# Six cross layers on one core: two more row quads biased on VectorE, and the fifth layer's products made one feature tile at a time

## The chip, the cores and the metric

The kernel runs on one core of one Trainium2 chip. The metric is the device time of one execution in microseconds, as the median of several runs; a single execution was recorded by the hardware profiler, and all views below are of that one.

## What is computed

A stack of six cross layers on 4096 rows with 416 features, all in bf16:

```python
B, F, D, L = 4096, 26, 16, 6          # features: F * D = 416
def reference(x0, ws, bs):            # x0 [4096, 416], ws [6, 416, 416], bs [6, 416]
    x = x0
    for l in range(ws.shape[0]):
        x = x0 * (x @ ws[l] + bs[l]) + x
    return x
```

Every layer multiplies by `x0` and adds the last `x`, so `x` is always `x0` times a factor: with c = 1 at first, each layer does c += x @ w + b and x = x0 * c. The kernel keeps that factor c (tiles `CM` and `CR`) and adds to it.

## The kernel before

**Layout.** In layers one to five everything is transposed: features on the partitions, rows along them. 416 features are three full tiles of 128 (m = 0, 1, 2) and a remainder of 32. The 4096 rows are two halves (s = 0, 1) of 2048, each four groups g of 512 columns. `XM0` is the transposed input, `XH` three rotating buffers for the transposed x of a half, `CM` the factor of the full tiles; the remainder lies in `XR` and `CR`, with the four groups of a half stacked on four blocks of 32 partitions. A feature tile of one half is 128 x 2048 elements, made as two pieces of 1024.

**A layer.** TensorE makes the sums of a tile (`mm_full`, L208, and the remainder's share in `mm_row`, L214) into two PSUM buffers of 1024 columns. ScalarE evicts each with the layer's bias (L187, or `evict`, L332, in layer five) into a buffer `t` (six of them). VectorE then does the addition to the factor (L188, or `add`, L340) and the product with `XM0` that gives the next x (L189, or `mul`, L344). There are six tiles a layer, called A, Bt, C (first half, m = 0 to 2) and Dt, E, F (second half).

**Layer five** is `feeding_layer` (L325). It has an order of its own, written out by hand from L381 to L427; `pin` keeps VectorE's instructions in the order of the text. Besides additions and products, it turns the factor back into rows for layer six: `rows_out` (L350) issues a DMA transpose of a finished tile of `CM` on SP's queue (`xl_dmat`, L231) into `XLrows`, and `rem_out` (L375) the same for the remainder by way of `scrR`, from where ScalarE copies it (`xl_rem`, L311). For the first half, `last_bias` (L347) adds the bias of layer six to the factor ahead of the transpose, after the tile's product was made. For the second half nothing is added, and the transpose is issued as soon as the additions are done.

**Layer six** (L450 on) works by rows: the output of 128 rows is a "unit" of 128 x 416 in PSUM. A quad q = (s, i) is the four units of i-th 128 columns of the four groups; so there are eight quads, and 32 units. Rounds of two quads each fill four PSUM tiles. `mm_q_rem` (L477) makes the remainder's share of a quad, four matmuls on four row groups (L480). In the second half (`if s`), four more matmuls of one row of ones with the bias (L484) put the bias into PSUM, as the transposed factor doesn't hold it. Then ScalarE casts the sums to `t` (L509), VectorE adds the rows of the factor (L511) and multiplies by `X0rows` (L499), and the output is issued on SP's queue (L500). At the very end, for the last three units, TensorE adds the factor itself by products with the identity (L472, L474), and the last unit is multiplied straight from PSUM and stored from ScalarE's queue.

SP's queue holds, in order of the text: the loads of the start, the eight transposes of layer five, and 22 of the 23 outputs.

Of the kernel before, what the change touches and what calls it, by code (L numbers as in the profile page):

```python
# [10 lines left out]
ALU = mybir.AluOpType  # L11
# [5 lines left out]
def kernel(  # L17
# [7 lines left out]
    nc = tc.nc  # L25
    B, D = x0.shape
    L = ws.shape[0]
# [4 lines left out]
    NS = 2  # L32
    NG = 4
    CW = 512
    SW = NG * CW
    NBT = B // P
    LL = L - 1
# [14 lines left out]
    WR = const.tile([P, L, D], BF16)  # L52
# [3 lines left out]
    bM = const.tile([P, NK, L], FP32)  # L56
    bR = const.tile([P, L], FP32)
    X0rows = big.tile([P, NBT, D], BF16)
    XLrows = big.tile([P, NBT, D], BF16)
    scrR = [big.tile([P, 4, P], BF16, name=f"scrR{s}") for s in range(NS)]  # L60
# [3 lines left out]
    XM0 = big.tile([P, NK, B], BF16, name="XM0")  # L64
    XH = [big.tile([P, NK, SW], BF16, name=f"XH{i}") for i in range(3)]
    XR = [big.tile([P, NS * CW], BF16, name=f"XR{i}") for i in range(3)]
    CM = big.tile([P, NK, B], BF16, name="CM")
    CR = big.tile([P, NS * CW], BF16, name="CR")

    def col0(s, g):  # L70
        return SW * s + CW * g
# [8 lines left out]
    def pin(ins):  # L80
        tc.keep_in_program_order(ins)
# [136 lines left out]
    def mm_rem(l, s, pr, cur, curR):  # L218
        for g in range(NG):
            nc.tensor.matmul(pr[32 * g:32 * g + 32, :], lhsT=WD[:, l, g, :], rhs=curR[:, CW * s:CW * s + CW],  # L220
                             start=True, stop=False, tile_position=(0, 32 * g))
        for k in range(NK):
            for g in range(NG):
                nc.tensor.matmul(pr[32 * g:32 * g + 32, :], lhsT=WM[:, l, k, NK * P:D], rhs=cur[s][:, k, CW * g:CW * g + CW],  # L224
                      start=False, stop=(k == NK - 1), tile_position=(0, 32 * g))
# [4 lines left out]
    def xl_dmat(s, k):  # L230
        nc.sync.dma_start_transpose(out=XLrows[:, 16 * s:16 * s + 16, 128 * k:128 * k + 128],  # L231
                                    in_=CM[:, k, SW * s:SW * s + SW])
# [73 lines left out]
    def xl_rem(s):  # L306
        dst = XLrows[:, 16 * s:16 * s + 16, NK * P:D].rearrange("p (g i) r -> p i g r", g=NG)
        src = scrR[s][:].rearrange("p i (g r) -> p i g r", g=NG)
        n = 4 if s else 2
        for i in range(0, 4, n):  # L310
            pin(nc.scalar.copy(dst[:, i:i + n], src[:, i:i + n]))  # L311

    def layer_products(l, n, tiles, pts, cur, curR, between):
        ta, tb = tiles[n], tiles[n + 1]
        pts[ta] = new_pts()
        for g in range(NG):
            mm_full(l, ta[0], ta[1], g, pts[ta], cur, True, False)
        mm_row(l, ta[0], ta[1], pts[ta], curR, False, True)
        pts[tb] = new_pts()
        mm_row(l, tb[0], tb[1], pts[tb], curR, True, False)  # L320
        between(ta)
        for g in range(NG):
            mm_full(l, tb[0], tb[1], g, pts[tb], cur, False, True)

    def feeding_layer(l, cur, curR, nxt, nxtR):  # L325
        tiles = [(s, m) for s in range(NS) for m in range(NK)]
        pts, ts = {}, {}

        def evict(t):
            for h in range(2):  # L330
                ts[t + (h,)] = tpool.tile([P, 2 * CW], BF16, name="t")
                nc.scalar.activation(ts[t + (h,)][:], pts[t][h][:].rearrange("p a b -> p (a b)"), ACT.Identity,  # L332
                                     bias=bM[:, t[1], l:l + 1], scale=1.0)

        def c_of(t, h):
            c0 = col0(t[0], 2 * h)
            return CM[:, t[1], c0:c0 + 2 * CW]

        def add(t, h):
            pin(nc.vector.tensor_tensor(out=c_of(t, h), in0=ts[t + (h,)][:], in1=c_of(t, h), op=ALU.add))  # L340

        def mul(t, h):
            c0 = col0(t[0], 2 * h)
            pin(nc.vector.tensor_tensor(out=nxt[t[0]][:, t[1], 2 * CW * h:2 * CW * h + 2 * CW], in0=c_of(t, h),  # L344
                                        in1=XM0[:, t[1], c0:c0 + 2 * CW], op=ALU.mult))

        def last_bias(c, bias):  # L347
            pin(nc.vector.tensor_scalar(out=c, in0=c, scalar1=bias, scalar2=None, op0=ALU.add))

        def rows_out(t):  # L350
            s, m = t
            if s == 0:
                last_bias(CM[:, m, 0:SW], bM[:, m, LL:L])
            xl_dmat(s, m)

        A, Bt, C, Dt, E, F = tiles
        layer_products(l, 0, tiles, pts, cur, curR, evict)
        evict(Bt)
        pr2 = psum.tile([P, 2, CW], FP32, tag="ps", name="pr2")
        for s in range(NS):  # L360
            mm_rem(l, s, pr2[:, s, :], cur, curR)
        tr = []
        for s in range(NS):
            tr.append(tpool.tile([P, 2 * CW], BF16, name="t"))
            for a in range(0, CW, CW // 2):
                nc.scalar.activation(tr[s][:, a:a + CW // 2], pr2[:, s, a:a + CW // 2], ACT.Identity, bias=bR[:, l:l + 1], scale=1.0)

        def rem(s, op):
            part = slice(CW * s, CW * s + CW)
            if op == ALU.add:  # L370
                pin(nc.vector.tensor_tensor(out=CR[:, part], in0=tr[s][:, 0:CW], in1=CR[:, part], op=op))
            else:
                pin(nc.vector.tensor_tensor(out=nxtR[:, part], in0=CR[:, part], in1=XR[0][:, part], op=op))

        def rem_out(s):  # L375
            part = slice(CW * s, CW * s + CW)
            if s == 0:
                last_bias(CR[:, part], bR[:, LL:L])
            nc.sync.dma_start_transpose(out=scrR[s][:], in_=CR[:, part])

        add(A, 0)  # L381
        mul(A, 0)
        add(A, 1)
        add(Bt, 0)
        mul(A, 1)
        rows_out(A)
        add(Bt, 1)
        mul(Bt, 0)
        rem(0, ALU.add)
        mul(Bt, 1)  # L390
        rem(0, ALU.mult)
        rem_out(0)
        rows_out(Bt)
        rem(1, ALU.add)
        rem_out(1)
        rem(1, ALU.mult)

        layer_products(l, 2, tiles, pts, cur, curR, evict)
        evict(Dt)
        add(C, 0)  # L400
        add(C, 1)
        mul(C, 0)
        mul(C, 1)
        rows_out(C)
        add(Dt, 0)
        add(Dt, 1)
        rows_out(Dt)
        mul(Dt, 0)
        mul(Dt, 1)

        def before_last(t):
            xl_rem(0)
            evict(t)

        layer_products(l, 4, tiles, pts, cur, curR, before_last)
        evict(F)
        add(E, 0)
        mul(E, 0)
        add(E, 1)
        rows_out(E)  # L420
        add(F, 0)
        mul(E, 1)
        add(F, 1)
        rows_out(F)
        mul(F, 0)
        mul(F, 1)
        xl_rem(1)  # L427

    cur, curR = XH[0:2], XR[1]
    for l in range(1, LL):  # L430
        nxt, nxtR = [[h for h in XH if h is not cur[0] and h is not cur[1]][0], cur[0]], XR[1 + (l % 2)]
        if l == LL - 1:
            feeding_layer(l, cur, curR, nxt, nxtR)
            cur, curR = nxt, nxtR
            break
        tiles = [(s, m) for s in range(NS) for m in range(NK)]
        pts = {}

        def finish(t):
            for h in range(2):  # L440
                ew_main(l, t[0], t[1], h, pts[t][h], nxt)

        for n in range(0, len(tiles), 2):
            layer_products(l, n, tiles, pts, cur, curR, finish)
            finish(tiles[n + 1])
            if n == 0:
                rem_pair(l, cur, curR, nxtR)
        cur, curR = nxt, nxtR

    l = LL  # L450
# [25 lines left out]

    def mm_q_rem(q, py, done):  # L477
        s, i = quads[q]
        for g in range(NG):
            nc.tensor.matmul(py[g][:, 0:D], lhsT=curR[32 * g:32 * g + 32, CW * s + 128 * i:CW * s + 128 * i + 128],  # L480
                             rhs=WR[32 * g:32 * g + 32, l, :], start=(g >= done), stop=(s == 0 and g < done),
                             tile_position=(32 * g, 0))
        for g in range(NG if s else 0):
            nc.tensor.matmul(py[g][:, 0:D], lhsT=ones[32 * g:32 * g + 1, :],  # L484
                             rhs=bLr[32 * g:32 * g + 1, :], start=False, stop=(g < done), tile_position=(32 * g, 0))

# [88 lines left out]
```

## Time and profile before

| what | us |
|---|---|
| median of three runs | 129.69 |
| runs, lowest to highest | 129.56 to 129.72 |
| the profiled execution | 129.56 |
| its span, first to last instruction | 127.8 |
| TensorE busy in the span | 123.0 |
| VectorE busy in the span | 102.3 |
| ScalarE busy in the span | 87.6 |

The span is what the profile shows; 1.76 us of the execution lie around it. Busy time is the time in which an engine's instructions ran; overlapping ones are counted once. Each row of the order of time has the start, the length, the engine, the line of the kernel, output and inputs by the program's names, the shape and how many instructions are merged in the row; in brackets stands the idle time of the engine ahead of it, and what ended it. PE is TensorE, DVE is VectorE, ACT is ScalarE, SPq the queue of SP. The granted clock of TensorE was 0.999 over the span.

### The profile page before, as it was taken

Reading aid. Unit: us, or ns where it says so; the run is one execution under the profiler, and the core shown is the slowest. Engines: PE = TensorE matmul, PEld = TensorE weight load, DVE = VectorE, ACT = ScalarE, POOL = GpSimd, SP = SyncE. Lnnn points to the kernel's source line nnn. Section 1 sums busy time; section 2 is a strip of 40 time slices with the busy share of each in tenths; the row PEclk is TensorE's granted clock in tenths of the full one; section 3 lists DMA queues with packets and bytes.
Section 4 is the critical chain, followed back from the end, with each engine's and each line's share of the span. In section 5 each row is a group of like instructions: output and inputs, shape, how many; then the busy total and the mean of one; then the engine's idle time right before and its main releaser. Section 6 shows DMA issues by size and latency. Waiting matters only on the chain.

```text
span 127.8 us, 3986 instructions
## 1 busy us (share of the span) xinstructions
PE 123.0 (96%) x1692; PEld 55.5 (43%) x1694; DVE 102.3 (80%) x199; ACT 87.6 (69%) x109; POOL 5.0 (4%) x18
## 2 busy tenths in 40 slices
PE   7999999999999999999999999999999999999980
PEld 3343343444444344534454434443545345445450
DVE  0123569974979898989898989898999999998990
ACT  0038866887858567858577859577859697669660
POOL 4004001400000000000000000000000000000000
PEclk9999999999999999999999999999999999999999
DMA  3999999999950000000000000000078999999964
GB/s 95 237 234 219 178 235 260 310 333 333 339 159 0 5 0 0 8 0 5 0 5 0 5 0 0 5 0 5 0 146 92 183 164 202 165 263 286 311 198 148
DMA packets 42230, 16.38 MB, mean 128 GB/s; under 512 B 31034, under 2 KB 42212, under 8 KB 42212
## 3 DMA queue, kind: packets, MB, share of 16 engines
q1 hardware_dynamic: 37432, 15.40, 52.9%
q10 hardware_dynamic: 4780, 0.72, 3.6%
q8 instruction: 13, 0.21, 0.7%
q14 instruction: 5, 0.04, 0.1%
HBM read 6.15 MB, written 3.41 MB: 75 GB/s over the span
## 4 chain that ended last, share of the span: by engine, by line
PE 90%; DMA 4%; ACTq 2%; DVEq 1%; issue 0%; ACT 0%; DVE 0%
PE pt L208 50%; PE py L468 12%; PE ph L240 11%; PE pt L214 5%; PE pr L224 5%; DMA xrig<-in_x_dram 4%; PE pr L220 2%; PE py L480 2%; PE ph L247 1%; PE py L462 1%; ACTq L86 1%; PE py L484 1%; DVEq L570 1%; ACTq L108 1%; ACT t L509 0%
## 5 line engine op out<-in xcount | busy, mean ns | idle before, releaser
L208 PE MATMUL pt<-XH,WM 128*32 128x512 bf16 x1152 | 65.2, 379 | 0.0
L187 ACT ACTIVATE t<-pt,bM 128x1024 bf16<-128x1024 f32 x36 | 37.1, 1114 | 13.7 <-PE pt L214 13.7
L208 PEld LDWEIGHTS <-WM 128*32 128x32 bf16 x1152 | 29.7, 97 | 33.8 <-issue 5.1
L188 DVE TENSOR_TENSOR CM<-t,CM 128x1024 bf16<-128x1024 bf16 x36 | 24.7, 687 | 4.2 <-ACT t L187 4.2
L189 DVE TENSOR_TENSOR XH<-CM,XM 128x1024 bf16<-128x1024 bf16 x36 | 24.9, 692 | 2.6
L509 ACT CAST t<-py 128x416 bf16<-128x416 f32 (+1 forms) x22 | 14.3, 648 | 4.5 <-PE py L468 2.1
L468 PE MATMUL py<-WM,XH 128*128 128x416 bf16 x90 | 17.0, 339 | 0.0
L240 PE MATMUL ph<-XM,WM 128*128 128x512 bf16 x70 | 16.3, 379 | 0.2
L332 ACT ACTIVATE t<-pt,bM 128x1024 bf16<-128x1024 f32 x12 | 12.4, 1114 | 4.2 <-PE pt L214 4.2
L181 ACT ACTIVATE CM<-ph,bM 128x1024 bf16<-128x1024 f32 x12 | 12.5, 1113 | 3.5 <-PE ph L247 3.5
L183 DVE TENSOR_TENSOR XH<-CM,XM 128x512 bf16<-128x512 bf16 x24 | 9.1, 439 | 3.6 <-ACT CM L181 3.6
L468 PEld LDWEIGHTS <-XH 128*128 128x128 bf16 x90 | 8.5, 98 | 7.5 <-issue 1.2
L240 PEld LDWEIGHTS <-WM 128*128 128x128 bf16 x72 | 6.8, 98 | 8.6 <-issue 1.1
L499 DVE TENSOR_TENSOR o<-t,X0rows 128x416 bf16<-128x416 bf16 (+1 forms) x22 | 9.9, 458 | 0.1
L511 DVE TENSOR_TENSOR t<-t,XLrows 128x416 bf16<-128x416 bf16 (+1 forms) x20 | 9.3, 468 | 0.6 <-ACT t L509 0.6
L340 DVE TENSOR_TENSOR CM<-t,CM 128x1024 bf16<-128x1024 bf16 x12 | 7.9, 685 | 0.3 <-ACT t L332 0.3
L344 DVE TENSOR_TENSOR XH<-CM,XM 128x1024 bf16<-128x1024 bf16 x12 | 8.0, 686 | 0.1
L214 PE MATMUL pt<-XR,WR 32*128 32x512 bf16 x96 | 7.3, 379 | 0.0
L224 PE MATMUL pr<-XH,WM 128*32 128x512 bf16 x96 | 6.6, 379 | 0.0
L196 ACT ACTIVATE t<-pr,bR 128x256 bf16<-128x256 f32 x12 | 4.7, 474 | 1.6 <-PE pr L224 1.6
L114 ACT ACT_TABLE_LOAD x1 | 1.3, 1283 | 6.1 <-DMA XM<-in_x_dram 6.1
L224 PEld LDWEIGHTS <-WM 128*32 128x32 bf16 x120 | 3.2, 97 | 3.2
(61 smaller groups left out, 58.2 us busy)
## 6 DMA issues: line engine op xcount, KB each, us to landing
X0rows<-in_x_dram SPq DMA_DIRECT2D x8, 312.0 KB, 7.0
out_dram<-o SPq DMA_DIRECT2D x9, 208.0 KB, 3.3
WM<-in_ws_dram SPq DMA_DIRECT2D x5, 312.0 KB
out_dram<-o SPq DMA_DIRECT2D x13, 104.0 KB, 1.9
X0rows<-in_x_dram SPq DMA_DIRECT2D x4, 208.0 KB, 6.4
WR<-in_ws_dram SPq DMA_DIRECT2D x4, 130.0 KB, 5.1
WM<-in_ws_dram ACTq DMA_DIRECT2D x1, 312.0 KB
XM<-in_x_dram SPq DMA_TRANSPOSE x8, 5.7
```

What stands on the lines that cost most here:

```text
L181: nc.scalar.activation(c, src, ACT.Identity, bias=bias, scale=1.0)
L187: nc.scalar.activation(t[:], src, ACT.Identity, bias=bias, scale=1.0)
L188: nc.vector.tensor_tensor(out=c, in0=t[:], in1=c, op=ALU.add)
L189: nc.vector.tensor_tensor(out=x, in0=c, in1=XM0[:, m, c0:c0 + 2 * CW], op=ALU.mult)
L208: nc.tensor.matmul(pts[g // 2][32 * q:32 * q + 32, g % 2, :], lhsT=WM[:, l, k, 128 * m + 32 * q:128 * m + 32 * q + 32], rhs=cur[s][:, k, C ...
L214: nc.tensor.matmul(pts[g // 2][:, g % 2, :], lhsT=WR[32 * g:32 * g + 32, l, 128 * m:128 * m + 128], rhs=curR[32 * g:32 * g + 32, CW * s:CW ...
L224: nc.tensor.matmul(pr[32 * g:32 * g + 32, :], lhsT=WM[:, l, k, NK * P:D], rhs=cur[s][:, k, CW * g:CW * g + CW], start=False, stop=(k == NK ...
L240: nc.tensor.matmul(pt[:, gl, :], lhsT=WM[:, 0, k, 128 * m:128 * m + 128], rhs=cur[:, k, c0:c0 + CW], start=(k == 0 and not after_row), sto ...
L332: nc.scalar.activation(ts[t + (h,)][:], pts[t][h][:].rearrange("p a b -> p (a b)"), ACT.Identity, bias=bM[:, t[1], l:l + 1], scale=1.0)
L468: nc.tensor.matmul(py[:, 0:D], lhsT=q_x(q, g, k), rhs=WM[:, l, k, :], start=((not closes) and k == 0), stop=(closes and not adds and k == ...
L499: pin(nc.vector.tensor_tensor(out=o[:, 0:n, :], in0=src, in1=X0rows[:, b, :], op=ALU.mult))
L509: nc.scalar.copy(tv, src)
```

## The change

Two things are changed together.

First, the bias of layer six. `rows_out` and `rem_out` now add it for the second half too, but there only to the first 256 columns of each group of 512 (quads i = 0 and 1), as a two-dimensional slice of four pieces of 256 for a full tile, and 256 columns for the remainder. `mm_q_rem` makes the bias matmuls for quads i = 2 and 3 of the second half alone. As the product needs the factor without that bias, `rows_out` of Dt, E and F and `rem_out` of the second half now come after the product of the tile (in the second half's remainder: after L373's product).

Second, the products. `mul` can be given a start and a number of 512-column groups. Tile A's product stays in two pieces; those of Bt, C, Dt, E and F are one instruction of 2048 columns each. The hand-written order around them is changed to fit.

```diff
-        def mul(t, h):
-            c0 = col0(t[0], 2 * h)
-            pin(nc.vector.tensor_tensor(out=nxt[t[0]][:, t[1], 2 * CW * h:2 * CW * h + 2 * CW], in0=c_of(t, h),
-                                        in1=XM0[:, t[1], c0:c0 + 2 * CW], op=ALU.mult))
+        def mul(t, h=0, n=2):
+            c0, w = col0(t[0], 2 * h), n * CW
+            pin(nc.vector.tensor_tensor(out=nxt[t[0]][:, t[1], 2 * CW * h:2 * CW * h + w], in0=CM[:, t[1], c0:c0 + w],
+                                        in1=XM0[:, t[1], c0:c0 + w], op=ALU.mult))
 
         def rows_out(t):
             s, m = t
-            if s == 0:
-                last_bias(CM[:, m, 0:SW], bM[:, m, LL:L])
+            c = CM[:, m, SW * s:SW * s + SW]
+            if s:
+                c = c.rearrange("p (g r) -> p g r", g=NG)[:, :, 0:CW // 2]
+            last_bias(c, bM[:, m, LL:L])
             xl_dmat(s, m)
 
         def rem_out(s):
-            part = slice(CW * s, CW * s + CW)
-            if s == 0:
-                last_bias(CR[:, part], bR[:, LL:L])
-            nc.sync.dma_start_transpose(out=scrR[s][:], in_=CR[:, part])
+            last_bias(CR[:, CW * s:CW * s + (CW // 2 if s else CW)], bR[:, LL:L])
+            nc.sync.dma_start_transpose(out=scrR[s][:], in_=CR[:, CW * s:CW * s + CW])
 
         add(Bt, 1)
-        mul(Bt, 0)
         rem(0, ALU.add)
-        mul(Bt, 1)
+        mul(Bt, 0, 4)
         rem(0, ALU.mult)
+        rem(1, ALU.add)
         rem_out(0)
         rows_out(Bt)
-        rem(1, ALU.add)
-        rem_out(1)
         rem(1, ALU.mult)
 
         add(C, 0)
         add(C, 1)
-        mul(C, 0)
-        mul(C, 1)
+        rem_out(1)
+        mul(C, 0, 4)
+        add(Dt, 0)
         rows_out(C)
-        add(Dt, 0)
         add(Dt, 1)
-        rows_out(Dt)
-        mul(Dt, 0)
-        mul(Dt, 1)
+        mul(Dt, 0, 4)
...
         add(E, 0)
-        mul(E, 0)
+        rows_out(Dt)
         add(E, 1)
+        mul(E, 0, 4)
+        add(F, 0)
         rows_out(E)
-        add(F, 0)
-        mul(E, 1)
         add(F, 1)
+        mul(F, 0, 4)
         rows_out(F)
-        mul(F, 0)
-        mul(F, 1)
...
     def mm_q_rem(q, py, done):
         s, i = quads[q]
+        biased = s == NS - 1 and i >= 2
         for g in range(NG):
             nc.tensor.matmul(py[g][:, 0:D], lhsT=curR[32 * g:32 * g + 32, CW * s + 128 * i:CW * s + 128 * i + 128],
-                             rhs=WR[32 * g:32 * g + 32, l, :], start=(g >= done), stop=(s == 0 and g < done),
+                             rhs=WR[32 * g:32 * g + 32, l, :], start=(g >= done), stop=(not biased and g < done),
                              tile_position=(32 * g, 0))
-        for g in range(NG if s else 0):
+        for g in range(NG if biased else 0):
```

## Prediction

> **What bounds the kernel now.** I read the page first (shares of the span, slices, chain), then a table of busy time by stretches for layers five and six, then the order of time on VectorE and on SP's queue, and last the rows around the matmuls that go.
>
> ```profile
> PE 123.0 (96%) x1692; PEld 55.5 (43%) x1694; DVE 102.3 (80%) x199; ACT 87.6 (69%) x109; POOL 5.0 (4%) x18
> ...
> DVE  0123569974979898989898989898999999998990
> ...
> PE 90%; DMA 4%; ACTq 2%; DVEq 1%; issue 0%; ACT 0%; DVE 0%
> ```
>
> By this page TensorE is the bound: 96% busy and 90% of the chain. But the DVE row of slices is full over the last thirty per cent of the span, and that is where the change lies. So I asked for the stretches one by one (columns: stretch, its length, then busy time of each engine).
>
> ```profile
> core 0: us, PE busy (x) PEld busy (x) DVE busy (x) ACT busy (x) POOL busy (x), PEclk, DMA share, GB/s
> ...
> 92.30:107.10 14.80, 14.80 (x244) 6.75 (x237) 14.66 (x27) 12.02 (x16) 0.00 (x0) 1.00 0.90 148
> 107.10:115.60 8.50, 8.50 (x66) 4.19 (x64) 7.87 (x17) 5.98 (x8) 0.00 (x0) 1.00 1.13 222
> 115.60:124.70 9.10, 8.39 (x68) 4.55 (x65) 9.03 (x28) 6.57 (x13) 0.00 (x0) 1.00 0.84 260
> ```
>
> From 92.30 us on VectorE is busy 14.66 of 14.80, 7.87 of 8.50 and 9.03 of 9.10 us. It has some 0.6 us to give in the middle stretch and next to none elsewhere; in the last stretch it is fuller than TensorE (8.39 of 9.10). Two engines are critical there, and TensorE leads only where VectorE waits for it.
>
> ```profile
> 107.15 1.08 DVE L511 TENSOR_TENSOR t<-t,XLrows 128x832 bf16<-128x832 bf16 x2
> ...
> 111.93 0.59 DVE L511 TENSOR_TENSOR t<-t,XLrows 128x832 bf16<-128x832 bf16 x1 [0.18 <-ACT t L509]
> ...
> 115.59 0.59 DVE L511 TENSOR_TENSOR t<-t,XLrows 128x832 bf16<-128x832 bf16 x1 [0.45 <-ACT t L509]
> ```
>
> VectorE ends layer five and begins layer six's additions at 107.15, when the first cast (105.04 to 105.92) has been ready for over a microsecond: it is late. It catches up by 111.93, where it waits 0.18 us for a cast, and again at 115.59 (0.45). After 115.59 no wait is marked to the end.
>
> ```profile
> 92.40 1.78 SPq L231 DMA_TRANSPOSE XLrows<-CM  x1
> 95.30 1.97 SPq L379 DMA_TRANSPOSE scrR<-CR  x1
> 97.36 2.01 SPq L231 DMA_TRANSPOSE XLrows<-CM  x1
> 99.47 1.58 SPq L379 DMA_TRANSPOSE scrR<-CR  x1
> 101.14 10.78 SPq L231 DMA_TRANSPOSE XLrows<-CM  x4
> 112.02 13.22 SPq L500 DMA_DIRECT2D out_dram<-o  x22
> ```
>
> SP issues the eight transposes and the 22 outputs in one row. From 95.30 to 125.24 it has hardly a gap, though the first output was computed by 108.74. What lies on this queue has its own pace.
>
> **The change, part by part.**
>
> *TensorE.* Quads 0 and 1 of the second half lose their bias matmuls: 8 of L484's 16, in two groups of four, both in the round that opens near 114 us.
>
> ```profile
> 114.30 0.35 PE L484 MATMUL py<-bLr,ones 1*128 1x416 bf16 x4
> 114.48 0.34 PE L480 MATMUL py<-WR,XR 32*128 32x416 bf16 x4
> 114.65 0.34 PE L484 MATMUL py<-bLr,ones 1*128 1x416 bf16 x4
> 114.70 1.47 ACT L509 CAST t<-py 128x832 bf16<-128x832 f32 x2 [0.69 <-PE py L484]
> ```
>
> One matmul lasts 335 ns, but the four of a group overlap on their row groups: the next group starts 0.18 us later. So the two groups are worth 0.18 + 0.175 = 0.35 us, and ScalarE's cast, which waits for the first of them, comes as much earlier. The rest of TensorE's work is unchanged. Layer six's first half needs the products of tiles A to C before 103.4 and has them by 99.1 (after: 98.9); the second half reads D to F near 113.8 and they are complete at 107.2 (after: below 108). No wait arises there.
>
> *VectorE, added.* Four bias additions. No row shows 1024 or 256 elements for this operation; L348 takes 753 ns for 2048 and 353 ns for 512, so 0.26 ns an element: about 486 and 287 ns. The next independent instruction starts 0.08 us before a row's end (95.15 to 95.81 is 0.66 for a 753 ns row), so in line they cost 0.40 and 0.20 us. Three and one: 1.40 us. Bounds for the strided 1024: 0.27 us from the 512 row below, 0.60 us from an L340 row of 1024 above (a rate of half). I take 0.40, as both rows of the same operation lie on its line; two-piece operands cost nothing visible in L511, whose 832 and 416 rows (587 and 371 ns) lie on one line with L340's 685 for 1024.
>
> *VectorE, merged.* Five pairs of 1024-element products become five of 2048. A pair costs 2 x 0.60 in line (101.00, 101.61, 102.21). L373 with 512 costs 0.34, so the slope is 0.26 per 512 and the long one 0.34 + 3 x 0.26 = 1.12, say 1.13. Bounds: 1.20 (nothing gained), 1.02 (slope alone). Gain 5 x 0.07 = 0.35 us.
>
> *VectorE, order.* An instruction right behind the one whose result it reads starts 0.12 us later (102.21 to 102.93 is 0.72, not 0.60). Four such places go (first E product, second remainder product, remainder bias, bias of C) and four come (products of D, E, F right behind their second addition, bias of F behind its product): zero. Casts of layer five don't gate it: E's and F's second evictions end near 102.6 and 104.7, their additions start near 103.0 and 105.8.
>
> Sum: 1.40 - 0.35 + 0 = **+1.05 us**; layer six's first addition starts at 108.2 instead of 107.15. From there 15 instructions of 0.503 lead to the one that started at 115.59: 108.2 + 7.54 = 115.74. Its cast comes 0.35 earlier and no longer matters. So the 0.8 us of waiting that this stretch has (0.18 + 0.45, and small ones of 0.1 to 0.2 in all) is eaten, and VectorE is 0.15 us late there. Then 8.09 us of instructions without a stop (115.59 to 123.40, and 0.28 more) lead to the last but one product: 123.83. Before it started at 123.84, since a cast ended at 123.82; that cast now comes 0.35 earlier. VectorE's end stays where it was.
>
> *SP's queue.* Order A, remainder 0, B, remainder 1, C, D, E, F stays. Remainder 0's transpose waits for a bias that now ends near 95.39 instead of 95.23, since the second remainder's addition stands ahead: +0.16. The others become ready at 96.1 (B), 97.8 (remainder 1), 100.2 (C), 103.1 (D), 105.9 (E) and 108.3 (F), all before the queue reaches them (97.36, 99.47, 101.14, 104.29, 106.12, 109.97). So the late bias of F has a cover of 1.6 us; without it, all outputs would wait for it. What is queued behind is the next transpose and then the outputs; VectorE's additions wait for the landing of C (106.08, needed at 108.2) and of F (114.31, needed at 115.74): met. Two transposes took far over the usual 1.6 to 2.0 us on SP (C 3.06, E 3.75), so the 0.16 may be swallowed by such a stall or go through to the outputs: 0 to +0.16, I take 0.08. ScalarE's copy of remainder 0 (98.72, landing 98.70) may wait 0.2 us, with 1.1 us of its own idle time behind it.
>
> Total: 0 on VectorE's end, +0.08 on the queue whose last output lands last (126.85): **+0.08 us**. The profiled execution took 129.56 us, 1.76 more than its span; it is the fastest of the three (median 129.69). So 129.64 on that execution, and **129.77** as a median.
>
> **The rivals.**
>
> *TensorE's saving arrives (faster).* If VectorE's added work were 0.5 to 0.6 us instead of 1.05 (bias at its lower bound, 3 x 0.13 less, products at theirs, 5 x 0.10 less, would do), the addition at 115.59 would follow the earlier cast and the tail would shift by up to 0.35 us, if SP's queue follows: 129.35 as a median. For it: the chain and the 96%. Against: VectorE's waits sum to only 0.8 us, and SP's last four outputs leave 0.48 us apart (123.39, 123.87, 124.36, 124.84), the first of them 0.19 us behind its product, so that the queue alone would keep some 0.2 of the 0.35. The Trainium skill (Perfetto Trace Analysis, Identifying the Most-Contended Engine) picks the engine with the highest occupancy to optimize first, while calling matmul busy time a poor measure; by occupancy this rival would be the forecast, and the stretches above contradict it for the end.
>
> *The strided bias runs at half the rate (slower).* At 0.60 us each, three cost 0.60 more; nothing is left to cover it once the 0.8 us are used, which is the point from which it decides: 129.77 + 0.6 = 130.37. For it: the trace has no such operand in this operation. Against: L511. The Trainium skill (VectorE: DVE Perf Modes, What auto-detection actually checks) ties the two-port modes to even or equal outermost dimensions; four pieces here would keep them, which no row of before can show.
>
> *The queue decides (slower).* SP's stream has stalls whose place may shift with the earlier matmuls; one output took 1.52 us at 115.88 where others take 0.45. One more of that kind costs up to 1.07 us, less what the lag behind VectorE returns: 130.1 to 130.8.
>
> **How the numbers follow.** Forecast 0.50 (own range 129.55 to 130.0), TensorE's saving 0.20, half rate 0.17, queue 0.13. A measurement tells 0.2% (0.26 us) from no change: faster than 129.43 holds most of the first rival, slower than 129.95 the two last and a tenth of the forecast. Faster 0.18, same 0.46, slower 0.36. Range: from the first rival's time to just past half rate, 129.3 to 130.45.
>
> **What would show it.** L484 x8; L344 as two rows of 1024 elements and five of 2048 near 1.22 us; L348 strided near 0.49 us; the first L511 near 108.2; no wait marked on VectorE near 112 and 115.6; SP's transposes at the same times within 0.2 us. Wrong if the first L511 starts before 107.8 (faster) or after 108.6 (slower), if a strided bias takes 0.6 us or more, or if an output on SP waits for F's transpose past 112.2.

## The result and the profile after

The changed kernel takes 129.85 us (median of 17 runs, 129.57 to 130.74); the kernel before takes 129.5 us beside it (17 runs, 129.13 to 129.81). The ratio is 1.0033, with an interval from 1.0019 to 1.0047: slower by 0.25 to 0.6 us. The profiled execution took 129.89 us with a span of 128.1, against 129.56 and 127.8 before.

The same three stretches of the changed kernel (stretch, its length, busy time of PE, PEld, DVE, ACT, POOL):

```profile
92.30:107.10 14.80, 14.80 (x244) 6.72 (x237) 14.49 (x25) 12.09 (x17) 0.00 (x0) 1.00 0.96 150
107.10:115.60 8.50, 8.50 (x60) 4.18 (x58) 8.41 (x16) 6.23 (x9) 0.00 (x0) 1.00 1.14 229
115.60:124.70 9.10, 8.07 (x66) 4.40 (x64) 9.10 (x30) 6.34 (x13) 0.00 (x0) 1.00 0.77 243
```

TensorE has shed its share: 8.07 us busy in the last stretch, not 8.39. VectorE is busy 8.41 of 8.50 and then 9.10 of 9.10 us; the 0.6 us of the middle stretch are gone. The order of time on VectorE, around the start of layer six and at the ninth addition of rows (L507 is what L511 was, L495 was L499):

```profile
105.60 0.48 DVE L348 TENSOR_SCALAR CM<-CM,bM 128x1024 bf16<-128x1024 bf16 x1
106.00 0.69 DVE L340 TENSOR_TENSOR CM<-t,CM 128x1024 bf16<-128x1024 bf16 x1
106.78 1.23 DVE L344 TENSOR_TENSOR XH<-CM,XM 128x2048 bf16<-128x2048 bf16 x1
108.05 0.49 DVE L348 TENSOR_SCALAR CM<-CM,bM 128x1024 bf16<-128x1024 bf16 x1
108.59 1.09 DVE L507 TENSOR_TENSOR t<-t,XLrows 128x832 bf16<-128x832 bf16 x2
...
116.12 0.59 DVE L507 TENSOR_TENSOR t<-t,XLrows 128x832 bf16<-128x832 bf16 x1
```

The first addition comes at 108.59 instead of 107.15, the ninth at 116.12 instead of 115.59, and the waits of 0.18 and 0.45 us ahead of the sixth and the ninth are gone. The cast of the ninth unit did come earlier, by TensorE's saving:

```profile
114.16 0.53 PE L476 MATMUL py<-WR,XR 32*128 32x416 bf16 x8
114.54 1.85 ACT L505 CAST t<-py 128x832 bf16<-128x832 f32 x3 [0.49 <-PE py L476]
```

It starts at 114.54, not 114.70, and its 0.85 us end long before 116.12: nobody waits for it. The chain of work that ended last was TensorE's for 90% of the span and VectorE's for 0%; now its line on the page is

```profile
PE 86%; DMA 4%; DVE 3%; ACTq 2%; issue 1%; ACT 0%; DVEq 0%
```

and from 119.6 us on, all but short pieces of it are VectorE's. On SP's queue the change shows little:

```profile
101.06 11.13 SPq L231 DMA_TRANSPOSE XLrows<-CM  x4
112.29 13.23 SPq L496 DMA_DIRECT2D out_dram<-o  x22
```

The outputs start 0.27 us later and end 0.28 later (125.52 against 125.24).

### The profile page after: what moved, and what is told of

Read it like the earlier page. It is cut to its first block, busy times and chain, and to the rows that moved or that the text cites. A ratio compares the mean times of both kernels' runs of the same rounds, so it can differ in the third digit from the quotient of the medians.

```text
span 128.1 us, 3968 instructions
## 1 busy us (share of the span) xinstructions
PE 122.5 (96%) x1684; PEld 55.3 (43%) x1686; DVE 102.9 (80%) x198; ACT 87.7 (68%) x109; POOL 5.6 (4%) x18
## 4 chain that ended last, share of the span: by engine, by line
PE 86%; DMA 4%; DVE 3%; ACTq 2%; issue 1%; ACT 0%; DVEq 0%
PE pt L208 50%; PE ph L240 11%; PE py L463 10%; PE pt L214 5%; PE pr L224 5%; DMA xrig<-in_x_dram 4%; DVE t L507 2%; PE pr L220 2%; PE ph L247 1%; PE py L476 1%; DVE o L495 1%; PE py L457 1%; ACTq L86 1%; ACTq L108 1%; ACT t L505 0%
## 5 line engine op out<-in xcount | busy, mean ns | idle before, releaser
L189 DVE TENSOR_TENSOR XH<-CM,XM 128x1024 bf16<-128x1024 bf16 x36 | 24.9, 692 | 2.6
L495 DVE TENSOR_TENSOR o<-t,X0rows 128x416 bf16<-128x416 bf16 (+1 forms) x22 | 9.9, 463 | 0.0
L507 DVE TENSOR_TENSOR t<-t,XLrows 128x416 bf16<-128x416 bf16 (+1 forms) x20 | 9.3, 470 | 0.1
L344 DVE TENSOR_TENSOR XH<-CM,XM 128x2048 bf16<-128x2048 bf16 (+1 forms) x7 | 7.5, 1070 | 0.4
```

The costliest lines, as they stand in the source:

```text
L189: nc.vector.tensor_tensor(out=x, in0=c, in1=XM0[:, m, c0:c0 + 2 * CW], op=ALU.mult)
L507: pin(nc.vector.tensor_tensor(out=tv, in0=tv, in1=XLrows[:, rows(q, g0, n), :], op=ALU.add))
```

## The experiments

The theory: **VectorE** sets the end of the changed kernel; layer five gives it more work than its waiting could hide, and TensorE's saving therefore buys nothing. The rivals: **TensorE** (its saving counts and something else lost more) and **SP's queue** (the outputs go at their own pace).

All traces start with some tenths of spread from the loads. So the times below are counted from layer five's first addition on VectorE in the same trace (at 88.28 before, 88.32 after): the first and ninth addition of rows in layer six, and the end of the last product (start and length of its row, less that start).

| kernel | first | ninth | last product ends | ratio to before (interval) |
|---|---|---|---|---|
| before | 18.87 | 27.31 | 36.44 | 1 |
| changed | 20.27 | 27.80 | 36.75 | 1.0033 (1.0019 to 1.0047) |
| e1_pe_alone | 18.87 | 27.11 | 36.08 | 0.9990 (0.9974 to 1.0007) |
| e2_ve_alone | 20.26 | 27.79 | 36.74 | 1.0037 (1.0025 to 1.0049) |
| e3_order_alone | 18.88 | 27.31 | 36.44 | 1.0000 (0.9991 to 1.0009) |
| e4_no_ve_bias | 18.88 | 27.11 | 36.08 | 0.9984 (0.9975 to 0.9994) |
| e6_halves | 19.75 | 27.27 | 36.22 | 0.9994 (0.9984 to 1.0004) |
| e7_dose | 21.69 | 29.22 | 38.16 | 1.0140 (1.0125 to 1.0155) |
| e10_fewer_gaps | 19.18 | 27.10 | 36.08 | 0.9984 (0.9971 to 0.9997) |
| e11_fewer_gaps_pe16 | 19.18 | 27.31 | 36.44 | 1.0000 (0.9988 to 1.0013) |

(In the last two, a bias addition stands behind the first addition; the second comes at 20.08 in both, at 20.78 in the changed kernel.)

### TensorE's part alone

```diff
# from before
-        for g in range(NG if s else 0):
+        biased = s == NS - 1 and i >= 2
+        for g in range(NG if biased else 0):
# and stop= of the matmuls ahead of them to fit
```

> The kernel before without the bias matmuls of the second half's quads 0 and 1, and with nothing added on VectorE instead (it leaves out layer six's bias for those two quads). TensorE theory (its chain sets the time): 0.35 us less, ratio 0.997. VectorE theory: the cast that VectorE waits 0.45 us for at 115.59 comes 0.35 earlier, the addition starts at 115.24, and the rest follows: also up to 0.35 less, ratio 0.997. Queue theory (SP's outputs run back to back from 112.0 whatever the products do): at most 0.15 less, ratio 0.999 to 1.000.

Measured: 0.9990, not clear of 1; 129.22 us against 129.41. The ninth addition comes only 0.20 earlier, the last product 0.36. The interval (up to 0.34 us less) reaches almost to the whole saving, and so hardly tells TensorE from queue here. What is new is the 0.20: of the two groups of four that went, one stands behind the ninth unit's last matmul.

### VectorE's part alone

```diff
# from after
-        biased = s == NS - 1 and i >= 2
+        biased = s == NS - 1
```

> The changed kernel with all 16 bias matmuls back (it adds layer six's bias twice in the two quads). VectorE theory: VectorE comes to layer six at 108.6 and then runs without a stop to the end, so 0.35 us more on TensorE is not felt: the time of the changed kernel, ratio 1.003 to the kernel before, first addition after the ninth cast still near 116.1. TensorE theory: the saving was real and hidden by another loss, so without it 0.35 us more than the changed kernel, ratio 1.006.

Measured: 1.0037 and the changed kernel's times on VectorE to 0.01 us, though TensorE ends 0.36 us later again. In the changed kernel, TensorE's saving is worth nothing. That removes the TensorE rival.

### Products and order alone, without the bias

```diff
# from after, with all 16 bias matmuls
-            last_bias(c, bM[:, m, LL:L])
+            if s == 0:
+                last_bias(c, bM[:, m, LL:L])
# rem_out likewise
```

> The changed kernel's merged products and order, but no bias on VectorE for the second half and all 16 bias matmuls on TensorE (the full computation). VectorE theory: 1.4 us of the added bias gone, so layer six's first addition near 107.2 as before, time as before, ratio 1.000. If the new order or the late transposes cost something of their own (queue theory), ratio 1.002 or more although VectorE is as early as before.

Measured: 1.0000, and VectorE's times those of before to 0.01 us. Merging five products was worth 5 x 0.07 = 0.35 us by the prediction; here it is worth nothing. What the merge gained, the order gave back: four products (here C's too, as no remainder's bias stands ahead of it) start 0.19 to 0.20 us later behind their additions than a free instruction would. The late transposes cost nothing of their own.

### TensorE's saving with the order, without the bias

The same edit on the changed kernel, with its eight bias matmuls.

> The changed kernel without the bias additions on VectorE for the second half (it leaves out layer six's bias for the two quads): merged products, new order and TensorE's saving. VectorE theory: first addition near 107.2, ninth cast 0.35 earlier, so 0.35 us less than before, ratio 0.997; it says that the added bias costs 0.8 us against this kernel. Queue theory: ratio 0.999 or more.

Measured: 0.9984, clear of 1, and 0.6 us (129.85 less 129.25) below the changed kernel. The four bias additions are the loss; 1.39 us of VectorE's time come and go between 18.88 and 20.27. But the 0.35 us less than before that the VectorE theory expected (0.997) lie outside the interval: less than the whole of TensorE's saving arrives.

### The bias on GpSimd

```diff
# last_bias is given the engine
-            last_bias(c, bM[:, m, LL:L])
+            last_bias(c, bM[:, m, LL:L], nc.gpsimd if s else nc.vector)
```

> The changed kernel with the three strided bias additions of the second half on GpSimd in place of VectorE (the full computation). VectorE theory: some 1.2 us leave VectorE, layer six's first addition starts near 107.4, and the time falls to that of the kernel without these additions, ratio 0.998 to 0.999 against the kernel before, as long as the transposes of D, E and F (issued at 104.2, 106.1 and 108.9 in the changed kernel) aren't held back by a slow GpSimd. Queue theory: each microsecond by which F's bias ends after 109 shifts the outputs by as much; at 2 us an addition the ratio would be 1.005 or more.

Measured: 1.0267 (1.0245 to 1.0289), 132.88 us. GpSimd's and VectorE's rows, from two views of one trace, and SP's:

```profile
102.74 3.13 POOL L348 TENSOR_SCALAR CM<-CM,bM 128x1024 bf16<-128x1024 bf16 x1 [76.61 <-DVE XH L344]
106.11 7.22 POOL L348 TENSOR_SCALAR CM<-CM,bM 128x1024 bf16<-128x1024 bf16 x2 [0.23 <-DVE XH L344]
```

```profile
102.47 2.21 DVE L340 TENSOR_TENSOR CM<-t,CM 128x1024 bf16<-128x1024 bf16 x2
...
107.32 1.87 DVE L344 TENSOR_TENSOR XH<-CM,XM 128x2048 bf16<-128x2048 bf16 x1
```

```profile
105.90 9.38 SPq L231 DMA_TRANSPOSE XLrows<-CM  x3
115.37 0.97 SPq L496 DMA_DIRECT2D out_dram<-o  x1
```

An addition takes over 3 us there (the spans of GpSimd are rough), so F's transpose comes late (issued at 113.35), and with it the first output: 115.37 instead of 112.29. VectorE's relief did not come: some of its rows grew, and its first addition of layer six stands at 20.38, counted as in the table, no earlier than in the changed kernel. What F's transpose holds back is VectorE's ninth addition, the first that reads the rows of the second half:

```profile
119.41 0.59 DVE L507 TENSOR_TENSOR t<-t,XLrows 128x832 bf16<-128x832 bf16 x1 [1.85 <-issue]
...
L507 DVEq EVENT_SEMAPHORE  x4: 21/35/3192, 107.4 to 116.2; - x4
```

(Again two views of one trace.) A wait instruction of this line, begun at 116.2, lasts 3192 ns, and the transpose has landed at 119.33. The ninth addition is at 30.68 instead of 27.80: 2.88 us, most of the 3.03 us lost. So F's late transpose decides here, as the prediction said it would once F's bias ends after the queue is free, and it does so by way of VectorE's wait as well as by the outputs behind it.

### Products of D, E and F in halves

```diff
-        mul(Dt, 0, 4)
+        mul(Dt, 0)
+        mul(Dt, 1)
# E and F likewise
```

> The changed kernel with the products of D, E and F in two pieces of 1024 again (the full computation). In the changed kernel each of these long products starts 0.78 us after the addition it follows, not 0.60, as it must wait for it to end; the first piece needs only the first addition. VectorE theory: 3 x 0.18 saved, 3 x 0.07 lost, so layer six's first addition 0.3 us earlier, near 108.3, and some 0.2 to 0.3 us less time: ratio 1.001 to 1.002. If merging was a gain, or VectorE isn't the bound: 1.003 or more.

Measured: 0.9994, no difference from before any more, and better than expected: first addition 0.52 us earlier than in the changed kernel (20.27 to 19.75), the last product 0.53.

```profile
105.73 0.69 DVE L340 TENSOR_TENSOR CM<-t,CM 128x1024 bf16<-128x1024 bf16 x1
106.33 1.29 DVE L344 TENSOR_TENSOR XH<-CM,XM 128x1024 bf16<-128x1024 bf16 x2
107.66 0.49 DVE L348 TENSOR_SCALAR CM<-CM,bM 128x1024 bf16<-128x1024 bf16 x1
108.06 1.09 DVE L510 TENSOR_TENSOR t<-t,XLrows 128x832 bf16<-128x832 bf16 x2
```

Against the rows of the changed kernel: the product starts 0.60 behind the addition (0.78 there), as its first half needs only the first addition. Three such places give 0.56 and cost 0.2 for the second pieces. And the first addition of layer six starts 0.40 behind F's bias (0.54 there).

### A dose: each bias addition twice

```diff
             last_bias(c, bM[:, m, LL:L])
+            if s:
+                last_bias(c, dz[:, 0:1])
```

> The changed kernel with each of the three strided bias additions followed by a second one of the same shape that adds zero (the full computation). VectorE theory: nothing is left to hide it, so 3 x 0.40 to 3 x 0.55 us come through whole: 1.2 to 1.6 us more than the changed kernel, ratio 1.0125 to 1.0155. TensorE or queue theory: less than half of that, ratio below 1.008.

Measured: 1.0140, that is 131.22 us, 1.37 more than the changed kernel. VectorE's first addition comes 1.42 later, the last product 1.41.

```profile
109.13 0.49 DVE L348 TENSOR_SCALAR CM<-CM,bM 128x1024 bf16<-128x1024 bf16 x1
109.65 0.48 DVE L348 TENSOR_SCALAR CM<-CM,dz 128x1024 bf16<-128x1024 bf16 x1
```

What VectorE is given in layer five, the kernel pays in full, and SP's queue moves with it: its last output is issued at 38.21, 1.41 later than in the changed kernel (36.80). Neither rival allows that.

### One more store from ScalarE's queue

```diff
# from e4_no_ve_bias
-            ..., nc.scalar if final and u == 7 else nc.sync,
+            ..., nc.scalar if final and u >= 6 else nc.sync,
```

> The kernel without bias on VectorE for the second half (it leaves out layer six's bias for two quads), and with the last but one output stored from ScalarE's queue like the last. Without that move the ratio was 0.9984, and SP issued its last output 0.70 us behind its product. Queue theory: that lag takes what TensorE's saving still could give; SP then ends 0.48 us earlier and the time falls by 0.1 to 0.3 us more, ratio 0.996 to 0.9975. VectorE theory alone: no further change, ratio 0.998 to 0.999.

Measured: 1.0005 (0.9992 to 1.0018), slower than both theories had it and, by the medians, than without the move. SP's last output was issued 0.51 us earlier (35.78 instead of 36.29, counted as in the table), but ScalarE's last 0.28 later (36.39 instead of 36.11). The move only shifted the end from one queue to the other. So this run doesn't say how much SP's lag takes of TensorE's saving.

### Fewer starts right behind a result, and TensorE's saving on top

```diff
# from e6_halves
-        rows_out(A)
         add(Bt, 1)
+        rows_out(A)
...
-        rows_out(F)
+        late.append(lambda: rows_out(F))
# late = [] at the start; in ew, behind the first addition of XLrows
+        while late:
+            late.pop()()
```

> The changed kernel with the products of D, E and F in two pieces (as in e6_halves, ratio 0.9994, first addition of layer six at 108.06), and two more starts right behind the result they read taken out: A's bias goes behind B's second addition, F's bias and transpose behind the first addition of layer six (the full computation). VectorE theory: 0.2 to 0.3 us fewer on VectorE and the same end of the transposes, so 0.1 to 0.25 us less than e6_halves: ratio 0.997 to 0.9985, faster than both kernels. Queue theory: SP's lag behind the last products keeps it, ratio 0.999 to 1.000.

Measured: 0.9984 (0.9971 to 0.9997), 129.22 us against 129.37: the full computation, 0.04 to 0.38 us faster than the kernel before, and faster than the changed one by more.

```profile
106.75 1.30 DVE L346 TENSOR_TENSOR XH<-CM,XM 128x1024 bf16<-128x1024 bf16 x2
107.95 0.60 DVE L512 TENSOR_TENSOR t<-t,XLrows 128x832 bf16<-128x832 bf16 x1
108.45 0.49 DVE L350 TENSOR_SCALAR CM<-CM,bM 128x1024 bf16<-128x1024 bf16 x1
108.85 0.60 DVE L512 TENSOR_TENSOR t<-t,XLrows 128x832 bf16<-128x832 bf16 x1
```

From the first addition of layer six on, every start is 0.40 or 0.50 behind the last one, with no gap; this trace began 0.45 us later than that of the changed kernel (88.77 against 88.32). The ninth addition and the last product now stand where they stand without any added bias (27.10 and 36.08, as in e4_no_ve_bias).

The same with all 16 bias matmuls:

```diff
# from e10_fewer_gaps
-        biased = s == NS - 1 and i >= 2
+        biased = s == NS - 1
```

> The same with all 16 bias matmuls on TensorE (it adds layer six's bias twice in two quads). It asks what TensorE's 0.35 us are worth once VectorE is about as early as before. VectorE theory with TensorE close behind: the ninth addition waits for its cast again (0.2 us or so), ratio 0.9995 to 1.0015, that is 0.15 to 0.35 us more than e10_fewer_gaps; in the changed kernel itself the same edit cost nothing. If TensorE's work is not felt here either: the ratio of e10_fewer_gaps.

Measured: 1.0000, 129.47 us, 0.25 more than with eight (the two intervals still overlap a little). VectorE comes to layer six as early as in the run above (second addition 20.08 in both), but the ninth is 0.21 later and the last product 0.36. The very edit that cost nothing in the changed kernel costs 0.36 at the last product here. At VectorE's end, TensorE's saving is real as soon as VectorE isn't late.

## Why the prediction came out as it did

The mechanism was the one forecast: VectorE, not TensorE, decides from layer five on, its waiting of 0.8 us is eaten, and TensorE's 0.35 us buy nothing. The size was too small: 0.08 us were forecast and 0.25 to 0.6 measured, inside the range, but slower, to which the prediction gave a chance of 0.36, and not its likeliest case, no change (0.46). That the forecast of 129.77 lies only 0.08 us from the measured 129.85 is luck: it was built on 129.69, the median of three runs, where the kernel before takes 129.5 beside the changed one, and the two errors nearly cancel.

- **Added and merged, right.** The rows of the changed kernel (line, form, count, then busy time and mean ns):

```profile
L344 DVE TENSOR_TENSOR XH<-CM,XM 128x2048 bf16<-128x2048 bf16 x5 | 6.1, 1223 | 0.3
...
L348 DVE TENSOR_SCALAR CM<-CM,bM 128x1024 bf16<-128x1024 bf16 x3 | 1.4, 483 | 0.0
```

  483 ns for the strided bias (486 taken) and 1223 for the long product. The rival of the half rate is out.
- **Order, wrong: the mis-sized term.** "Four such places go and four come: zero" took 0.12 us for each. Those that came are dearer: the products start 0.78 to 0.80 behind the addition they need, where 0.60 is the step without a wait (0.18, 0.20, 0.18), F's bias 0.13 later than a free one, and the first addition of layer six 0.14 later, a place that was not on the list. Sum 0.83; those that went, 0.46. That is +0.37, and 1.05 + 0.37 = 1.42 against 1.40 measured. The dear products wait for two semaphores: a separate wait instruction for VectorE's own last result stands ahead of them. The first product of E in the kernel before has none and starts 0.72 behind its addition; but the first product of A, in the same trace, has one and starts 0.80 behind:

```profile
88.28 0.69 DVE L340 TENSOR_TENSOR CM<-t,CM 128x1024 bf16<-128x1024 bf16 x1 [0.29 <-ACT t L332]
89.08 0.69 DVE L344 TENSOR_TENSOR XH<-CM,XM 128x1024 bf16<-128x1024 bf16 x1
...
102.21 0.69 DVE L340 TENSOR_TENSOR CM<-t,CM 128x1024 bf16<-128x1024 bf16 x1
102.93 0.69 DVE L344 TENSOR_TENSOR XH<-CM,XM 128x1024 bf16<-128x1024 bf16 x1
```

  So the higher price could be read before. What the first addition of layer six lost its 0.14 to stays open: in e6_halves the same short bias and two wait instructions stand ahead of it, and it starts 0.40 behind. e6_halves closed this gap and those of the products, and in e3_order_alone such gaps ate the merge.
- **The ninth addition, partly wrong.** Its cast was to come 0.35 us earlier; it came 0.20, one group of four. It made no difference to the changed kernel, since VectorE was later than either.
- **VectorE's end, the consequence.** With 0.4 us more, the 0.15 us of lateness at the ninth addition became 0.49 (27.80 less 27.31), and the end 0.31 instead of 0. From there the sum held: 8.09 us behind 116.12 is 124.21, and the last but one product starts at 124.19.
- **SP's queue, right in being no cause.** C, D and E left within 0.11 us of before, and F left at 108.92 instead of 109.97, right behind E and 0.4 us after its bias had ended: the bias held nothing up. But F's row took 3.27 us instead of 1.96, so the outputs started 0.27 later, at 112.29, just past the 112.2 that the prediction had named as a sign of being wrong. Behind that start the queue still waits for VectorE's results 19 times, 7.2 us in all, so its late start is not what the kernel lost, and in e7_dose it follows VectorE. The 0.08 taken for the queue was not to be seen apart.

What stays open: by the last product TensorE's saving is 0.36 us, by the medians of e1, e4 and e10 some 0.15 to 0.2, with intervals that reach down to it in e10 alone. The traces suggest that the outputs' queue keeps the rest. SP's last output is issued, counted as in the table, at 36.56 before and 36.72 in e1; at 36.33 in e3 and 36.29 in e4; at 36.35 in e11 and 36.12 in e10. Of the 0.36 us, none, 0.04 and 0.23 arrive there. But these are single executions, and that of e1 was the longest of its twelve; e8, which was to test it, did not settle it.

## What to carry to other kernels

An engine's share of the whole span hides a last third in which another engine has no time left; read the waits of that engine by stretches before work is moved to it, and count them against the work. In an order written by hand, price each instruction that starts right behind the result it needs: merging two pieces can make an instruction wait that half of it would not have had to, and that cost more here (0.18 to 0.20 us) than the merge gained (0.07). When a saving shows nothing, try it again with the other engine relieved: here it was 0.36 us at the last product.

## What the runs showed of the hardware

- On VectorE an independent instruction starts 0.08 us before the row of the one ahead ends; one that needs its result, 0.04 to 0.12 us after it ends. The Trainium skill (Perfetto Trace Analysis, DVE / Act Engine Instruction) tells of the two cases: a row ends with the acknowledged write, the semaphore is seen after that, and the next instruction may begin to read before. The rows here agree, and give the price of 0.12 to 0.20 us in line.
- GpSimd took 3.1 to 3.7 us for the strided addition that VectorE does in 0.48. Beside it some of VectorE's instructions were longer (a product 1.87 us instead of 1.23, two additions 2.21 instead of 1.29), but a product of 1.23 us that ran almost wholly beside the first of them was not. The Trainium skill (SBUF — State Buffer, SBUF: two separate sides) says of the ports that the two share that the later one blocks for the whole of the other's instruction; here VectorE lost some 0.6 to 0.9 us at a time, not the whole 3 us.
